# The inputs' first transform as plain-float32 products on two 64-row halves, placed around the response products

## The chip, the cores and the metric

One core of one Trainium2 chip runs the whole kernel. The metric is the device time of one execution in microseconds; lower is better. The kernel before takes 1110.36 us (median of three runs, 1110.23 to 1110.42).

TensorE is called PE below, its weight loads PEld, VectorE DVE, ScalarE ACT, GpSimd POOL and SyncE SP, as in the profile. The queues of these engines run in order.

## The reference

The layer normalizes its input once and adds three things:

```python
x = A_u                                   # 1 x 2048 x 576
xn = _layernorm(x, axis=-1)
return x + _A_ref(xn, ...) + _B_ref(xn, B_w1, B_w2)
# _B_ref: silu(xn @ w1) @ w2,  w1 576 x 4608, w2 4608 x 576
# _A_ref: K[d,l] = Re sum_n C[d,n] exp(dt[d] A[d,n] l) dt[d] B[d,n]
#         y[:,d] = causal convolution of xn[:,d] with K[d,:], plus xn * Dskip
```

So there is a feed-forward branch (two large products with a SiLU between them), and a convolution of 2048 steps per channel, which the reference does with a Fourier transform of length 4096.

## The kernel before, in words

**Feed-forward branch** (`ffn`, lines 257 to 446). The rows are worked in two halves of 1024, each half in two blocks of 512; the 4608 hidden columns in nine chunks of four tiles of 128. `up` (line 321) makes one 128 x 512 tile of the hidden layer from 14 products (lines 331 to 333), then ACT takes the SiLU (line 339) and a rounded copy (line 340), and DVE the remainder (line 342). `down` (line 344) multiplies back in 24 products of 288 columns for each 128 rows (line 357), and DVE adds the result to `acc` (line 361). Every operand is split into a high and a low part of type float32r, and three of the four part products are made.

**Convolution branch** (`side`, line 863, a generator that `weave`, line 33, advances beside the feed-forward steps at fractions of the whole). It goes in stages:

- Layer norm, transposes, preparation of the exponentials (up to about 160 us).
- `kgen` (line 584), 36 chunks of 16 channels: ACT and DVE make tables `S` and `C` of damped sines and cosines (lines 653 to 676). At every second chunk (odd `i`) PE makes the responses from two chunks' tables, 64 plain-float32 products of 64 columns on 128 x 32 column tiles (`kp`, line 696). ACT copies them out (`kt`, line 703). Eight plain-float32 products of 128 columns on 64-row halves then make the first transform of the responses (`z`, line 711, stationary `kt`, moving `f1`), ACT copies the result into `stage` (line 719), and every second time it goes to DRAM.
- `spread` (line 145) makes the first transform of the normalized inputs in the same stretch of time. It is advanced one step by each chunk of `kgen` from the third on (lines 920 to 923). A step takes one of 16 tiles `j` and one half `m` of its rows: ACT rounds 64 rows to float32r into `sp` (line 156), DVE puts the remainder into the other 64 rows (line 157), and for each of two column halves of 288, PE makes two products (lines 161 and 162) with the high and the low part of a doubled matrix `s1`. ACT copies the result to `u1` (line 163), and POOL issues its store to `d1u` (line 164).
- `spectral` (line 730) and `tail` (line 785) do the rest of the convolution (`mm3`, line 821; `add_conv`, line 838, with products `py` of 64-row halves on 64 x 32 tiles, line 847).

**What sets the order.** The tile framework's scheduler orders each engine's queue when the program is built; `high_priority` moves an instruction ahead, and `behind` (line 142, `issue_after`) keeps it behind a named one. What is built is a fixed queue for each engine. The pool `pss` has three PSUM buffers for all small products of the convolution branch; `up` of line 918 has one buffer for `xr`, `u1` and `sp`.

Of the kernel before, what the change touches and what calls it, by code (L numbers as in the profile page):

```python
# [11 lines left out]
F32 = mybir.dt.float32  # L12
F32R = mybir.dt.float32r
# [6 lines left out]
P = 128  # L20
L = 2048
D = 576
NS = 128
FF = 4608
NJ = 16
NKT = 4
HD = D // 2
# [16 lines left out]
def kernel(  # L44
# [11 lines left out]
    w1: bass.AP,  # L56
    w2: bass.AP,
    cident: bass.AP,
    cs1: bass.AP,
    cf1: bass.AP,  # L60
    cm23: bass.AP,
    cs4: bass.AP,
# [3 lines left out]
    nc = tc.nc  # L66
# [73 lines left out]
    pins = {}  # L140

    def behind(ins):
        return tc.issue_after(ins) if ins is not None else nullcontext()

    def spread(up):

        s1 = up.tile([P, 2, P], F32R, name="s1", bufs=1)
        nc.gpsimd.dma_start(s1, cs1)
        for j in range(NJ):
            src = up.tile([P, D], F32, tag="xr", name="xr")  # L150
            nc.sync.dma_start(src, dxn[:, j])
            for m in range(2):
                lo, hi = slice(64 * m, 64 * m + 64), slice(64 - 64 * m, 128 - 64 * m)
                u1 = up.tile([P, D], F32, tag="u1", name="u1")
                sp = up.tile([P, D], F32R, tag="sp", name="sp")
                nc.scalar.copy(sp[lo, :], src[lo, :])
                nc.vector.tensor_sub(sp[hi, :], src[lo, :], sp[lo, :])
                for h in range(2):
                    hs = slice(h * HD, (h + 1) * HD)
                    pu = pss.tile([P, 512], F32, tag="pss", name="pu")  # L160
                    nc.tensor.matmul(pu[:, :HD], s1[:, 0, :], sp[:, hs], start=True, stop=False)  # L161
                    nc.tensor.matmul(pu[:, :HD], s1[:, 1, :], sp[:, hs], start=False, stop=True)  # L162
                    nc.scalar.copy(u1[:, hs], pu[:, :HD])
                nc.gpsimd.dma_start(
                    d1u.rearrange("(p m j) d -> m j p d", m=2, j=NJ)[m, j], u1)
                yield j

    def load_x(j, pool, tag, engines):
# [412 lines left out]
            v.tensor_mul(wt[:, :, k + 1], wt[:, :, k], ex[:, 3 * D:])  # L581
        nc.sync.dma_start(dmag, wt)

    def kgen():
        fT, phiT = kf["f"], kf["phi"]
        with tc.tile_pool(name="kg", bufs=1) as kg:
            CH = 8
# [58 lines left out]
            for i in range(NCK):  # L646
                th = nxt
                pk, ak = pw[:, i % 2], al[:, :, i % 2]
                c65 = kg.tile([P, W, 65], F32, tag="c65", name="c65")
                S = kg.tile([P, W, 96], F32, tag="S", name="S", bufs=2)  # L650
                C = kg.tile([P, W, 96], F32, tag="C", name="C", bufs=2)
                mag = C
                nc.scalar.activation(c65, th, AF.Identity, bias=magic)  # L653
                nc.vector.scalar_tensor_tensor(th, c65, MAGIC, th, op0=ALU.subtract, op1=ALU.subtract)  # L654
                nc.scalar.activation(c65, th, AF.Abs)  # L655
                nc.scalar.activation(th, th, AF.Sin, scale=TWO_PI)
                nc.scalar.activation(c65, c65, AF.Sin, scale=-TWO_PI, bias=halfpi)
                for g in range(2):
                    gs = slice(g * CH, (g + 1) * CH)
                    nc.vector.tensor_mul(  # L660
                        mag[:, gs, 0:32].rearrange("n d (x y) -> n d x y", y=4),
                        pk[:, gs, 0, :].unsqueeze(3).broadcast_to([P, CH, 8, 4]),
                        ak[:, g].unsqueeze(2).broadcast_to([P, CH, 8, 4]))
                nc.vector.tensor_mul(
                    mag[:, :, 32:96].rearrange("n d (x y) -> n d x y", y=8),
                    pk[:, :, 1, :].unsqueeze(3).broadcast_to([P, W, 8, 8]),
                    pk[:, :, 2, :].unsqueeze(2).broadcast_to([P, W, 8, 8]))
                if i + 1 < NCK:
                    nxt = head(i + 1)
                    if i % 2 == 1:  # L670
                        al = powers(i + 1)
                for dst, t, sg in ((S, th, -1.0), (C, c65, 1.0)):
                    ov3 = dst.rearrange("n d (x y) -> n d x y", y=32)[:, :, 0:3:2, :]
                    mv3 = mag.rearrange("n d (x y) -> n d x y", y=32)[:, :, 0:3:2, :]
                    nc.vector.tensor_mul(ov3, t[:, :, 0:64].rearrange("n d (x y) -> n d x y", y=32), mv3)
                    nc.vector.scalar_tensor_tensor(dst[:, :, 32:64], t[:, :, 64:32:-1], sg, mag[:, :, 32:64],  # L676
                                                   op0=ALU.mult, op1=ALU.mult)
                tabs.append((S, C))
                if i % 2 == 0:
                    yield (i + 1) / NCK  # L680
                    continue

                kp = pss.tile([P, 512], F32, tag="pss", name="kp")
                first = None
                for e in (1, 0):
                    S, C = tabs[e]
                    for gl in range(2):
                        for gp_ in range(2):
                            o = e * 256 + (gl * 2 + gp_) * 64
                            for q in range(4):  # L690
                                ch = gp_ * CH + gl * 4 + q
                                dst = kp[32 * q:32 * q + 32, o:o + 64]
                                begins = e == 1 and gl == 0 and gp_ == 0
                                with tc.high_priority(), behind(None if begins else first):
                                    for n, t in enumerate((C, S)):
                                        mm = nc.tensor.matmul(dst, t[:, ch, :32], t[:, ch, 32:],  # L696
                                                              start=begins and n == 0, stop=True,
                                                              tile_position=(0, 32 * q), skip_group_check=True)
                                if begins:
                                    first = mm.ins  # L700
                tabs = []
                kt = kg.tile([P, 512], F32, tag="kt", name="kt")
                nc.scalar.copy(kt, kp)

                z = [pss.tile([P, 512], F32, tag="pss", name="z") for _ in range(2)]
                first = None
                for eg in range(4):
                    for h in (1, 0):
                        rows = slice(64 * h, 64 * h + 64)
                        with tc.high_priority(), behind(first):  # L710
                            mm = nc.tensor.matmul(z[h][:, eg * P:(eg + 1) * P], kt[rows, eg * P:(eg + 1) * P], f1[rows],  # L711
                                                  start=True, stop=True, tile_position=(64 * h, 0))
                        first = first or mm.ins
                r = (i - 1) % NRUN
                if r == 0:
                    stage = kg.tile([P, 64, NRUN * CH], F32, tag="stage", name="stage")
                sv = stage[:, :, r * CH:(r + 2) * CH].rearrange("p k (e h c) -> p h e k c", h=2, c=2)
                for h in range(2):
                    nc.scalar.copy(sv[:, h], z[h].rearrange("p (e k c) -> p e k c", e=4, c=2))
                if r == NRUN - 2:  # L720
                    d0 = (i // NRUN) * NRUN * CH
                    kv = d1k.rearrange("(k n) (g d) -> g n k d", n=64, g=2)
                    for gp_ in range(2):
                        nc.sync.dma_start(kv[gp_, :, :, d0:d0 + NRUN * CH], stage[gp_ * 64:(gp_ + 1) * 64])
                yield (i + 1) / NCK
# [137 lines left out]
    def side():  # L863
# [3 lines left out]
        with tc.tile_pool(name="kf", bufs=1) as kfp:  # L867
# [49 lines left out]
            nc.sync.dma_start(vt, cv)  # L917
            with tc.tile_pool(name="up", bufs=1) as up:
                sp = spread(up)
                for n, at in enumerate(kgen()):  # L920
                    if n > 1:
                        next(sp, None)
                    yield marks[0] + at * (marks[1] - marks[0])
                for _ in sp:
                    pass
# [31 lines left out]
def _constants():  # L957
# [2 lines left out]
    n1 = np.arange(32)  # L960
    th = 2 * np.pi * np.outer(n1, k1 + 0.25) / 32
    cs = np.stack([np.cos(th), np.sin(th)], 2)
    s1 = np.zeros((2, 2, 32, 32, 2, 2), f8)
    f1 = np.zeros((2, 2, 32, 32, 2, 2), f8)
    for q in range(2):
        s1[:, q, :, :, :, q] = cs
        f1[:, q, :, :, :, q] = cs
    s4 = np.broadcast_to(cs.transpose(2, 1, 0) / L, (2, 2, 32, 32)).reshape(P, 32)
    s1 = np.stack(_hi_lo(s1.reshape(P, P)), 1)
    f1 = f1.reshape(P, P)  # L970
    n2 = np.arange(64)
    k2 = np.arange(64)
# [17 lines left out]
    v = np.broadcast_to(v, (P, 69))  # L990
    r = {
        "cident": np.eye(P),
        "cs1": s1,
        "cf1": f1,
        "cm23": m23,
        "cs4": s4,
# [26 lines left out]
```

## Time and profile before

| | |
|---|---|
| time, median of 3 runs | 1110.36 us |
| the profiled execution: span from the first to the last instruction | 1108.2 us |
| PE busy | 1102.2 us, 99% |
| DVE busy | 916.6 us, 83% |
| ACT busy | 706.9 us, 64% |
| POOL busy | 72.1 us, 7% |
| PE products (instructions in the trace) | 9167 |
| granted TensorE clock | full in every slice |

The profile gives the profiled execution no time besides its span; the median of the runs is 2.16 us above that.

A product is recorded from where it starts to where its result is out, so the records of successive products overlap, and the mean duration of one is more than the time that it takes up on PE. That time, called its turn below, is read from the starts of successive products, or from a piece of the chain of waits divided by its count. One plain-float32 product makes two records of weight load and two of product, called its two passes.

### The profile page before, as it was taken

The numbers are of one execution on the slowest core, as the hardware profiler recorded it, in microseconds if no ns is written. First come the engines' busy times: TensorE is split into PE (matmuls) and PEld (weight loads), VectorE is DVE, ScalarE is ACT, GpSimd is POOL, SyncE is SP. The second block draws the span as 40 slices with busy tenths as digits, with TensorE's granted clock in tenths as the row PEclk, the third lists the DMA queues.
The fourth block names the chain that finished last, engine by engine and source line by source line (L and its number), as shares of the span: only waits on it lengthen the run. The fifth ranks groups of instructions, "written<-read, shape, count | busy, mean of one in ns | idle before, by whom it ended". The sixth has DMA issues, their size and how long they took to land.

```text
span 1108.2 us, 22917 instructions
## 1 busy us (share of the span) xinstructions
PE 1102.2 (99%) x9167; PEld 997.5 (90%) x9167; DVE 916.6 (83%) x1543; ACT 706.9 (64%) x1222; POOL 72.1 (7%) x129
## 2 busy tenths in 40 slices
PE   9999999999999999999999999999999999999998
PEld 7989998899998899899999989999999999999887
DVE  7799899999999999999999737787778778784433
ACT  4564466676677676677867536877777878774210
POOL 1100000000000000011000000000000000000111
PEclk9999999999999999999999999999999999999999
DMA  9745512525252525264744173554544455434983
GB/s 270 190 123 160 152 50 61 120 73 131 77 121 83 116 72 118 77 174 154 206 122 103 45 179 109 162 167 123 156 145 152 138 149 170 129 107 127 241 224 87
DMA packets 175755, 148.56 MB, mean 134 GB/s; under 512 B 111088, under 2 KB 142592, under 8 KB 175520
## 3 DMA queue, kind: packets, MB, share of 16 engines
q1 hardware_dynamic: 165328, 112.63, 38.7%
q0 software_dynamic: 9568, 33.62, 9.6%
q8 instruction: 72, 1.18, 0.5%
q10 hardware_dynamic: 752, 0.85, 0.3%
q14 instruction: 35, 0.29, 0.1%
HBM read 102.53 MB, written 44.61 MB: 133 GB/s over the span
## 4 chain that ended last, share of the span: by engine, by line
PE 98%; DMA 1%; DVE 1%; SPq 0%; issue 0%; DVEq 0%
PE po L357 42%; PE ph L331 35%; PE kp L696 3%; PE ph L332 3%; PE ph L333 3%; PE pu L826 2%; PE pb L826 2%; PE pk L826 2%; PE z L711 2%; PE pu L161 1%; PE py L847 1%; DMA acc<-in_A_u_dram 1%; PE pu L162 1%; PE pt L124 0%; DVE w1l L295 0%; PE ptk L490 0%
## 5 line engine op out<-in xcount | busy, mean ns | idle before, releaser
L357 PE MATMUL po<-w2l,gh 128*128 128x288 f32 x1152 | 338.5, 295 | 0.0
L357 PE MATMUL po<-w2h,gl 128*128 128x288 f32 x1152 | 336.4, 295 | 0.0
L357 PE MATMUL po<-w2h,gh 128*128 128x288 f32 x1152 | 336.1, 295 | 0.0
L357 PEld LDWEIGHTS po<-w2h,gh 128*128 128x128 f32 x1152 | 215.2, 188 | 7.7 <-issue 2.8
L357 PEld LDWEIGHTS po<-w2l,gh 128*128 128x128 f32 x1152 | 215.9, 188 | 5.1 <-issue 0.5
L357 PEld LDWEIGHTS po<-w2h,gl 128*128 128x128 f32 x1152 | 215.4, 188 | 0.9
L339 ACT ACTIVATE gf<-ph 128x512 f32<-128x512 f32 (+1 forms) x148 | 86.4, 584 | 143.8 <-PE ph L333 134.8
L331 PE MATMUL ph<-xh,w1l 128*128 128x512 f32 (+1 forms) x592 | 161.3, 385 | 0.0
L331 PE MATMUL ph<-xh,w1h 128*128 128x512 f32 (+1 forms) x592 | 161.3, 387 | 0.0
L331 PE MATMUL ph<-xl,w1h 128*128 128x512 f32 (+1 forms) x592 | 161.1, 385 | 0.0
L361 DVE TENSOR_TENSOR acc<-po,acc 128x288 f32<-128x288 f32 x288 | 126.2, 451 | 37.0 <-PE po L357 35.6
L342 DVE TENSOR_TENSOR gl<-gf,gh 128x512 fp32r<-128x512 f32 (+1 forms) x148 | 99.0, 672 | 64.6 <-ACT gh L340 63.8
L331 PEld LDWEIGHTS ph<-xh,w1l 128*128 128x128 f32 x592 | 108.0, 188 | 20.0
L331 PEld LDWEIGHTS ph<-xl,w1h 128*128 128x128 f32 x592 | 107.9, 188 | 19.8
L331 PEld LDWEIGHTS ph<-xh,w1h 128*128 128x128 f32 x592 | 104.5, 188 | 16.7 <-ACT x L133 0.5
L340 ACT CAST gh<-gf 128x512 fp32r<-128x512 f32 (+1 forms) x148 | 89.5, 608 | 9.5 <-PE po L357 6.6
L653 ACT ACTIVATE c<-th,magic 128x1040 f32<-128x1040 f32 x36 | 42.1, 1168 | 37.9 <-DVE C L676 28.0
L655 ACT ACTIVATE c<-th 128x1040 f32<-128x1040 f32 x36 | 38.7, 1075 | 33.6 <-DVE th L654 33.6
L314 ACT CAST w2h<-w2r 128x576 fp32r<-128x576 f32 x72 | 47.0, 671 | 17.7 <-PE po L357 14.9
L295 DVE TENSOR_TENSOR w1l<-w1r,w1h 128x640 fp32r<-128x640 f32 x72 | 56.9, 817 | 0.2
L332 PE MATMUL ph<-x,w1h 128*128 128x512 f32 (+1 forms) x148 | 57.0, 386 | 0.0
L333 PE MATMUL ph<-x,w1l 128*128 128x512 f32 (+1 forms) x148 | 56.9, 385 | 0.0
(185 smaller groups left out, 1828.8 us busy)
## 6 DMA issues: line engine op xcount, KB each, us to landing
w2r<-in_B_w_dram SPq DMA_DIRECT2D x72, 288.0 KB, 3.8
w1r<-in_B_w_dram SPq DMA_DIRECT2D x35, 512.0 KB, 3.8
d1u<-u POOLq DMA_DIRECT2D x32, 288.0 KB, 2.5
d1k<-stage SPq DMA_DIRECT2D x18, 512.0 KB, 6.8
ur<-d1u SPq DMA_DIRECT2D x32, 288.0 KB, 3.7
kr<-d1k SPq DMA_DIRECT2D x32, 288.0 KB, 2.9
d<-yo POOLq DMA_DIRECT2D x32, 288.0 KB, 4.0
ys<-d SPq DMA_DIRECT2D x32, 288.0 KB, 11.8
```

The lines of the kernel that those rows point to most:

```text
L295: pins["w1l"] = nc.vector.tensor_sub(l1, src, h1).ins
L314: pins["w2h"] = nc.scalar.copy(h2, r2).ins
L331: nc.tensor.matmul(ph, w[:, kt, :], v[:, kt, a:e], start=n + kt == 0, stop=False)
L332: nc.tensor.matmul(ph, h1[:, 4, :], x4[:, a:e], start=False, stop=False)
L333: pins["pe"] = nc.tensor.matmul(ph, l1[:, 4, :], x4[:, a:e], start=False, stop=True).ins
L339: nc.scalar.activation(gf, ph, AF.Silu)
L340: pins["gh"] = nc.scalar.copy(gh, gf).ins
L342: pins["gl"] = nc.vector.tensor_sub(gl, gf, gh).ins
L357: pins["pe"] = nc.tensor.matmul(po[:, :HD], G[blk, t][g][:, js], W2[half, c, t][w][:, hs], start=n == 0, stop=n == 3 * FT - 1).ins
L361: nc.vector.tensor_add(acc[j][:, hs], po[:, :HD], acc[j][:, hs])
L653: nc.scalar.activation(c65, th, AF.Identity, bias=magic)
L826: nc.tensor.matmul(dst, st, mv[:, hs], start=n == 0, stop=n == 3 * len(terms) - 1)
```

## The change

`s1` and its load, the float32r split of the inputs (`sp`) and the paired high and low products go. Each tile `j` is now multiplied as it is, in plain float32, by the matrix `f1` that the response transform uses: rows 0 to 63 (`m` = 0) and rows 64 to 127 (`m` = 1) are two products of 64 rows by 128 columns with 288 moving columns, at tile positions 0 and 64, into two PSUM buffers. A step of `spread` is now one column half `h` of one `j` (32 steps as before), and holds one such pair. `u1` holds both `m` and gets two buffers.

`kgen` now advances `spread` itself: one step ahead of the run of `kp` products and one behind it, at every odd `i` from 3 on. `behind` puts the first pair after the latest feed-forward product, the run after the first pair, and the second pair after the run.

```diff
     def spread(up):
-        s1 = up.tile([P, 2, P], F32R, name="s1", bufs=1)
-        nc.gpsimd.dma_start(s1, cs1)
         for j in range(NJ):
             src = up.tile([P, D], F32, tag="xr", name="xr")
             nc.sync.dma_start(src, dxn[:, j])
-            for m in range(2):
-                lo, hi = slice(64 * m, 64 * m + 64), slice(64 - 64 * m, 128 - 64 * m)
-                u1 = up.tile([P, D], F32, tag="u1", name="u1")
-                sp = up.tile([P, D], F32R, tag="sp", name="sp")
-                nc.scalar.copy(sp[lo, :], src[lo, :])
-                nc.vector.tensor_sub(sp[hi, :], src[lo, :], sp[lo, :])
-                for h in range(2):
-                    hs = slice(h * HD, (h + 1) * HD)
-                    pu = pss.tile([P, 512], F32, tag="pss", name="pu")
-                    nc.tensor.matmul(pu[:, :HD], s1[:, 0, :], sp[:, hs], start=True, stop=False)
-                    nc.tensor.matmul(pu[:, :HD], s1[:, 1, :], sp[:, hs], start=False, stop=True)
-                    nc.scalar.copy(u1[:, hs], pu[:, :HD])
-                nc.gpsimd.dma_start(
-                    d1u.rearrange("(p m j) d -> m j p d", m=2, j=NJ)[m, j], u1)
+            u1 = up.tile([P, 2, D], F32, tag="u1", name="u1", bufs=2)
+            for h in range(2):
+                hs = slice(h * HD, (h + 1) * HD)
+                pu = [pss.tile([P, 512], F32, tag="pss", name="pu") for _ in range(2)]
+                last = pins["small"]
+                for m in (1, 0):
+                    rows = slice(64 * m, 64 * m + 64)
+                    with tc.high_priority(), behind(last):
+                        mm = nc.tensor.matmul(pu[m][:, :HD], f1[rows], src[rows, hs], start=True, stop=True,
+                                              tile_position=(64 * m, 0))
+                    last = pins["small"] = mm.ins
+                for m in range(2):
+                    nc.scalar.copy(u1[:, m, hs], pu[m][:, :HD])
+                if h:
+                    for m in range(2):
+                        nc.gpsimd.dma_start(d1u.rearrange("(p m j) d -> m j p d", m=2, j=NJ)[m, j], u1[:, m])
                 yield j
...
+                pins["small"] = pins["pe"]
+                if i > 1:
+                    next(sp, None)
+                first = pins["small"]
                 kp = pss.tile([P, 512], F32, tag="pss", name="kp")
-                first = None
...
-                                with tc.high_priority(), behind(None if begins else first):
+                                with tc.high_priority(), behind(first):
...
                 nc.scalar.copy(kt, kp)
-
+                pins["small"] = mm.ins
+                if i > 1:
+                    next(sp, None)
                 z = [pss.tile([P, 512], F32, tag="pss", name="z") for _ in range(2)]
...
-                for n, at in enumerate(kgen()):
-                    if n > 1:
-                        next(sp, None)
+                for at in kgen(sp):
                     yield marks[0] + at * (marks[1] - marks[0])
```

More of the change, by code (lines that the diff above doesn't have):

```diff
@@ L58 @@
     cident: bass.AP,
-    cs1: bass.AP,
     cf1: bass.AP,
@@ L582, in natural, with kgen @@
         nc.sync.dma_start(dmag, wt)
-    def kgen():
+    def kgen(sp):
         fT, phiT = kf["f"], kf["phi"]
@@ L962, in _constants @@
     cs = np.stack([np.cos(th), np.sin(th)], 2)
-    s1 = np.zeros((2, 2, 32, 32, 2, 2), f8)
     f1 = np.zeros((2, 2, 32, 32, 2, 2), f8)
     for q in range(2):
-        s1[:, q, :, :, :, q] = cs
         f1[:, q, :, :, :, q] = cs
     s4 = np.broadcast_to(cs.transpose(2, 1, 0) / L, (2, 2, 32, 32)).reshape(P, 32)
-    s1 = np.stack(_hi_lo(s1.reshape(P, P)), 1)
     f1 = f1.reshape(P, P)
@@ L992, in _constants @@
         "cident": np.eye(P),
-        "cs1": s1,
         "cf1": f1,
```

## The prediction

> **What bounds the kernel now.** I read the page first, for the busy shares, and then the chain of waits by line.
>
> ```profile
> span 1108.2 us, 22917 instructions
> PE 1102.2 (99%) x9167; PEld 997.5 (90%) x9167; DVE 916.6 (83%) x1543; ACT 706.9 (64%) x1222; POOL 72.1 (7%) x129
> ...
> by line: PE po L357 41.7%; PE ph L331 35.4%; PE kp L696 3.2%; PE ph L332 3.0%; PE ph L333 2.9%; PE pu L826 2.3%; PE pb L826 2.3%; PE pk L826 2.3%; PE z L711 1.8%; PE pu L161 1.1%; PE py L847 0.9%; DMA acc<-in_A_u_dram 0.8%; PE pu L162 0.8%;
> ```
>
> The chain is nearly all PE. A PE that is 99% busy may still hide short waits, so I asked for the stretch in which the change lies (160 to 645 us: PE, PEld, DVE, ACT and POOL busy, granted clock, DMA) and for the list of waits of PE.
>
> ```profile
> 160.00:645.00 485.00, 485.00 (x5149) 437.53 (x5149) 461.71 (x690) 334.62 (x504) 21.52 (x39) 1.00 0.40 107
> ...
> PE pz L879 <- DVE zero L874: 1.3, 1, 1.3
> PE pt L124 <- DVE xn L202: 0.4, 2, 0.2
> ```
>
> In those 485 us PE has no idle time, at the full clock (1.00); the two waits are of the start. DVE works for 461.7 us of it and ACT for 334.6, but PE waits for neither. So here time is won or lost only in PE's own queue: by the turns of products, by changes of tile mode, and by waits that the change adds.
>
> **Prices.** Two pieces of the chain in order of time, the timeline of PE around one visit to the 64-row mode, the same around one group of `py`, and the durations (min/median/max) of lines 711 and 847.
>
> ```profile
> 365.29 3.18 PE po L357 x24
> 368.70 2.74 PE ph L331 x12
> ...
> 174.23 0.39 PE L331 MATMUL ph<-xh,w1h 128*128 128x512 f32 x1
> 174.55 1.16 PE L711 MATMUL z<-f,kt 64*128 64x128 f32 x16
> 175.64 0.40 PE L161 MATMUL pu<-sp,s 128*128 128x288 f32 x1
> 175.88 0.30 PE L162 MATMUL pu<-sp,s 128*128 128x288 f32 x1
> ...
> 1080.49 0.29 PE L357 MATMUL po<-w2h,gl 128*128 128x288 f32 x1
> 1080.71 1.22 PE L847 MATMUL py<-ys,s 64*32 64x288 f32 x32
> 1081.86 0.73 PE L331 MATMUL ph<-xh,w1h 128*128 128x512 f32 x2
> ...
> L711 PE MATMUL z<-f,kt x288: 272/272/374, 174.5 to 643.0; 64*128 64x128 f32 x144
> ...
> L847 PE MATMUL py<-ys,s x256: 402/403/428, 1032.0 to 1097.0; 64*32 64x288 f32 x128
> ```
>
> - *A float32r product of 288 columns* has a turn of 3.18 / 24 = 0.1325 us, one of 512 columns 2.74 / 12 = 0.228.
> - *A visit to 64-row mode.* The 512-column product of 174.23 has had its turn at 174.46. L162 starts at 175.88; had L161 had one plain turn before it, PE would have been free for L161 at 175.75. So the visit cost 1.29 us.
> - *What of it is streaming.* The 16 records are eight products of two passes. The last record starts at 174.55 + 1.16 - 0.27 = 175.44. The first took 0.374 instead of 0.272, 0.10 of waiting for its weights. If the two halves run side by side there are eight rounds, seven of them between 174.65 and 175.44: 0.113 us each. That is 128 columns in 0.113, about half the rate of float32r (512 columns in 0.228), which fits a plain-float32 pass; one after another each record would have half of that, the full float32r rate. The durations decide: 128 to 288 columns lengthen a record by 403 - 272 = 131 ns, 0.82 ns a column, and float32r takes (0.228 - 0.1325) / 224 = 0.43 ns. So a pass has half the float32r rate, and the halves do run side by side.
> - *A switch.* Eight rounds are 0.90 of the 1.29 us. The other 0.39 is entering and leaving, 0.195 each: PE stands between the last product of one mode and the first of the next, and the first product's weights are not there ahead of it (0.10).
> - *A pass of 288 columns* in 64-row mode: 0.113 + 0.131 = 0.244 us. The `py` group checks it. It has 16 products on eight tiles, so four rounds. From 1080.49 + 0.1325 = 1080.62 to the second `ph` product (1081.86 + 0.73 - 0.39 = 1082.20) less a turn of 0.228, it cost 1.35; four rounds are 0.98, and 0.37 is left for two switches.
>
> **The change, part by part.**
>
> *Removed from PE:* 64 L161 and 64 L162, 128 x 0.1325 = 17.0 us. That their chain share (1.1% + 0.8% of 1108.2, 21.1 us) is more comes from L161 standing behind `z` in 17 rounds and taking over the leaving of it; the next product will take that over.
>
> *Added to PE, streaming:* 64 plain-float32 products of 64 rows. In the built order of the changed kernel 31 of the 32 pairs stand together and one is parted by eight feed-forward products, so there are 33 stretches of two passes: 33 x 2 x 0.244 = 16.1 us. At this point the change is about even: two passes at half the rate, two products at a time, against two products at full rate.
>
> *Added to PE, switches:* this decides. Counted in the built orders, the tile mode of PE's queue changes 96 times before and 145 times after. `kp` needs 128 x 32, the pairs 64 x 128, the feed-forward 128 x 128. Only 8 of the 16 first pairs lie directly against the run (14 to 77 feed-forward products stand between in the others), 15 second pairs begin directly behind it, and three `z` groups are now parted in two. A first pair that stands free costs two switches; a pair against the run costs one more than the run alone. 49 x 0.195 = 9.6 us.
>
> The trace has no border between the 64-row mode and `kp`'s. Below, such a border could cost nothing (the float32 work runs on); above, as much as a whole visit's overhead, 0.39. There are 23 of them (8 + 15). I take 0.195, as `z` shows for a change of rows, for both its directions; the ends are -4.5 and +4.5 us. The Trainium skill (TensorEngine Tiling (Array Packing), Key Properties) says that changing the tiling mode, not just the tile, drains TensorE. By that rule all 23 borders pay and the sum stays as it is; the trace agrees where it can be seen, with 0.39 us for a visit, and no run here yet shows that border.
>
> Another rule bears on the removal. The skill's page TensorE: Matmul & The Clock Gate (Back-to-back issue gap) gives N / 2.4 + 2.5 ns, an estimate of 122.5 ns for 288 columns, by which 15.7 us would go and the sum would be 1.3 us higher; the chain shows 132.5 ns, and that decides.
>
> *Removed elsewhere:* 32 roundings on ACT, 32 subtractions on DVE, one load on POOL.
>
> ```profile
> L156 ACT CAST sp<-xr 64x576 fp32r<-64x576 f32 x32 | 21.5, 673 | 6.0 <-DMA xr<-dxn 2.9 <-PE pu L162 2.7
> L157 DVE TENSOR_TENSOR sp<-xr,sp 64x576 fp32r<-64x576 f32 x32 | 24.1, 753 | 1.0
> L163 ACT COPY u<-pu 128x288 f32<-128x288 f32 x64 | 24.2, 400 | 10.5 <-PE pu L162 10.4
> ```
>
> That is 21.5 us of ACT and 24.1 us of DVE, worth nothing while PE has no idle time to give back. The 64 copies to `u1` (0.40 each), the 16 loads of `xr` on SP and 32 stores on POOL stay.
>
> *Added waits.* The second pair stands behind the run in PE's queue and needs the buffers of the first pair, so ACT's two copies of that pair. Behind it on PE are some 17 feed-forward products and `z`; all of them would stand too. I looked at how far ahead ACT and DVE are there, around the run at 222 us (timelines of DVE, ACT, PE; then the chain).
>
> ```profile
> 217.67 0.69 DVE L676 SCALAR_TENSOR_TENSOR C<-c,C 128x512 f32<-128x512 f32 x1
> ...
> 218.45 1.17 ACT L653 ACTIVATE c<-th,magic 128x1040 f32<-128x1040 f32 x1 [0.85 <-DVE C L676]
> 223.79 1.06 ACT L656 ACTIVATE th<-th 128x1040 f32<-128x1040 f32 x1
> 228.14 0.58 ACT L703 COPY kt<-kp 128x512 f32<-128x512 f32 x1
> ...
> 222.03 0.34 PE L696 MATMUL kp<-C 128*32 128x64 f32 x8
> ...
> 224.09 4.97 PE po L357 x36
> ```
>
> The run lasts from 222.03 to 224.09, 2.06 us. The built order of ACT mostly has the L653 operation (1.17) and the two copies (0.80) between: 1.97 us, covered even if L653 begins only when the first pair is done; in the trace it began 3.6 us ahead of the run. I cost this wait at nothing; without the cover it is the first rival. The tables were done at 218.36, 3.7 us ahead, so `kp`'s own wait has slack. On SP the load of the next `xr` now waits for PE's second pair instead of DVE; the table bases and weight loads queue behind it, but the tile is wanted only a round later (18 rounds in the stretch of 485 us, 27 us each), so nothing.
>
> **Sum:** 16.1 + 9.6 - 17.0 = +8.7 us. The profiled span of 1108.2 becomes 1116.9; with the 2.16 us by which the median of 1110.36 lies above that span, **1119.1 us**.
>
> **Rivals.**
>
> 1. *PE waits for ACT at the second pairs.* For it: the `kt` copy began 4.05 us after its run had ended, at 228.14, since ACT was working off its queue. Against: the copies stand ahead of the long sines. If ACT comes to the copies one such operation (1.06) late, 1.97 + 1.06 - 2.06 = 0.97 us are lost; at five to fifteen pairs that is 4.9 to 14.6 us: 1124.0 to 1133.7.
> 2. *Borders with `kp` are free:* 23 x 0.195 = 4.5 us less, 1114.6. For it: no row shows such a border. Against: both modes differ in rows and columns.
> 3. *The pairs don't run side by side,* so the change doesn't do what it says: 31 x 0.488 = 15.1 us more, 1134.2. Against: the eight rounds of `z`.
> 4. *Not slower: PE goes into and out of the 64-row mode for nothing,* weights loaded ahead. With all 49 switches at 0 the sum is 16.1 - 17.0 = -0.9, 1109.5 us. It decides at (2.2 + 0.9) / 49 = 0.06 us a switch. Against: 0.195 in `z`, which also goes from and to float32r products.
>
> **How the numbers follow.** The forecast, 1116.5 to 1122 with small waits, has 0.70; rival 1 0.13; rival 2 0.08; rival 3 0.03; rival 4 0.04, and 0.02 is for a gain that no row shows. 0.2%, about 2.2 us, is what a measurement here can tell from no change. Only rival 4 lies within it: faster 0.02, same 0.04, slower 0.94. The range takes in the forecast, rival 2 and the low end of rival 1: 1114.5 to 1124.0 leaves out just under 2 in 10.
>
> **What would show it.** Right: PE still without idle time between 160 and 645 us; the pair's two starts within some 10 ns and its first record about 0.10 us longer than its second pass's 0.40; a free pair's visit of 0.88 us (0.488 + 0.39), a pair against the run adding 0.68. Wrong: starts half a microsecond apart (rival 3); PE idle ahead of the second pair with ACT as releaser (rival 1); a `kp` border well under 0.2 us (rival 2); the feed-forward products slower or faster than 0.1325 and 0.228 us, which I take as unchanged.

## The result, and the profile after

The changed kernel takes **1123.26 us** (median of four runs, 1122.72 to 1123.62); the kernel before took 1110.31 us beside it (four runs, 1110.23 to 1110.42). The ratio is 1.0115, with a 95% interval of 1.0103 to 1.0127: 12.95 us slower, inside the forecast's range, 4.2 us above its value and above the narrower 1116.5 to 1122 that had most of the chance. The profiled execution took 1123.62 us, its span 1121.8.

First the page of the kernel after: the span, the busy shares, the chain by line.

```profile
span 1121.8 us, 22820 instructions
...
PE 1114.9 (99%) x9167; PEld 994.4 (89%) x9167; DVE 892.1 (80%) x1511; ACT 688.2 (61%) x1190; POOL 71.4 (6%) x128
...
PE po L356 37%; PE ph L330 31%; PE ph L332 3%; PE ph L331 3%; PE kp L698 2%; PE pu L830 2%; PE pb L830 2%; PE pk L830 2%; PE z L715 2%; PE pu L157 1%; PE py L851 1%; DMA acc<-in_A_u_dram 1%; DVE acc L360 1%; DMA xl<-dxt 1%; DVE th L653 1%
```

PE is 99% busy as before. Lines of the code have moved: the pair is L157 now, `z` L715, `kp` L698, the feed-forward products L330 to L332 and L356. The same stretch by time (PE, PEld, DVE, ACT, POOL busy, clock, DMA):

```profile
160.00:645.00 485.00, 484.93 (x4950) 422.80 (x4949) 432.45 (x650) 310.35 (x463) 21.41 (x39) 1.00 0.41 106
```

And all waits of PE that the trace lists in the kernel after:

```profile
PE pt L123 <- DVE xn L201: 1.3, 2, 1.1
PE pz L883 <- DVE zero L878: 1.3, 1, 1.3
```

PE still has no idle time in the stretch and the clock is full; DVE is busy for 29 us less there and ACT for 24, and PE gains nothing by it. (The operations taken out were 24.1 and 21.5 us; the rest is work that now lies later.) The stretch now holds 4950 product records where it held 5149, out of 9167 in both kernels: the same count takes longer in PE's own queue. Where, the timeline of PE shows; each row is a run of equal records with its start, its length and its count.

```profile
188.36 0.29 PE L356 MATMUL po<-w2h,gl 128*128 128x288 f32 x1
188.58 0.76 PE L157 MATMUL pu<-xr,f 64*128 64x288 f32 x4
189.27 0.50 PE L330 MATMUL ph<-xl,w1h 128*128 128x512 f32 x1
189.60 0.62 PE L330 MATMUL ph<-xh,w1l 128*128 128x512 f32 x2
...
201.25 0.29 PE L356 MATMUL po<-w2l,gh 128*128 128x288 f32 x1
201.47 1.49 PE L715 MATMUL z<-f,kt 64*128 64x128 f32 x16
202.89 0.40 PE L356 MATMUL po<-w2h,gl 128*128 128x288 f32 x1
203.13 0.29 PE L356 MATMUL po<-w2l,gh 128*128 128x288 f32 x1
...
220.59 0.29 PE L356 MATMUL po<-w2h,gl 128*128 128x288 f32 x1
220.81 0.76 PE L157 MATMUL pu<-xr,f 64*128 64x288 f32 x4
221.50 0.34 PE L698 MATMUL kp<-C 128*32 128x64 f32 x8
...
223.49 0.76 PE L157 MATMUL pu<-xr,f 64*128 64x288 f32 x4
224.18 0.50 PE L332 MATMUL ph<-x,w1l 128*128 128x512 f32 x1
224.51 0.29 PE L356 MATMUL po<-w2h,gh 128*128 128x288 f32 x1
...
359.49 0.29 PE L356 MATMUL po<-w2l,gh 128*128 128x288 f32 x1
359.72 1.16 PE L715 MATMUL z<-f,kt 64*128 64x128 f32 x8
360.80 0.40 PE L356 MATMUL po<-w2h,gl 128*128 128x288 f32 x1
361.04 0.30 PE L356 MATMUL po<-w2h,gh 128*128 128x288 f32 x1
```

A visit is read as in the prediction: from the end of the last full product's turn to the second full product, less a turn.

- *A free pair* (188.58): from 188.36 + 0.1325 = 188.49 to 189.60 - 0.228 = 189.37, so 0.88 us.
- *A pair, the run, a pair* (220.81): from 220.72 to 224.51 - 0.228 = 224.28, so 3.56 us. A run alone took 39.53 us in 18 visits before, 2.20 each. Each pair against the run adds 0.68.
- *A `z` group* (201.47): from 201.38 to 203.13 - 0.1325 = 203.00, so 1.61 us. Before it was 1.29 for the same 16 records.
- *Half a `z` group* (359.72, eight records): from 359.62 to 360.91, 1.29 us. Half the products cost as much as the whole group did, and the other half comes later, at 362.63, for as much again.

All visits between 160 and 700 us, summed the same way, are 62.72 us before (`kp` 39.53, `z` 23.19) and 92.81 after (`kp` and the pairs 64.09, `z` 28.72). With the 17.0 us that went, that is 92.81 - 62.72 - 17.0 = **+13.1 us**, against 12.95 measured. The spans differ by 13.6; 0.9 of that is the wait of `pt` in the first 20 us (1.3 us, 0.4 before), long before the first pair.

So `z`, which the change does not touch, costs 5.5 us more. In the queue as built, 10 of its 18 groups go on alternating between rows 64 to 127 (H) and rows 0 to 63 (l). Five run H H H l H l l l, at 1.61 us (in the trace the second half starts 0.33 us behind the first, against 0.007 where they alternate, and that late start is the whole 0.32); three are parted into H H H H and, later, l l l l, at twice 1.29. 5 x 0.32 + 3 x 1.29 = 5.5.

### The profile page after: what moved, and what is told of

It is laid out like the page before. It is cut to its first block, busy times and chain, and to the rows that moved or that the text cites. A ratio compares the mean times of both kernels' runs of the same rounds, so it can differ in the third digit from the quotient of the medians.

```text
span 1121.8 us, 22820 instructions
## 1 busy us (share of the span) xinstructions
PE 1114.9 (99%) x9167; PEld 994.4 (89%) x9167; DVE 892.1 (80%) x1511; ACT 688.2 (61%) x1190; POOL 71.4 (6%) x128
## 4 chain that ended last, share of the span: by engine, by line
PE 86%; DVE 6%; issue 4%; DMA 2%; ACT 1%; POOL 0%; SPq 0%; DVEq 0%; POOLq 0%
PE po L356 37%; PE ph L330 31%; PE ph L332 3%; PE ph L331 3%; PE kp L698 2%; PE pu L830 2%; PE pb L830 2%; PE pk L830 2%; PE z L715 2%; PE pu L157 1%; PE py L851 1%; DMA acc<-in_A_u_dram 1%; DVE acc L360 1%; DMA xl<-dxt 1%; DVE th L653 1%
## 5 line engine op out<-in xcount | busy, mean ns | idle before, releaser
L356 PE MATMUL po<-w2h,gh 128*128 128x288 f32 x1152 | 337.6, 296 | 0.0
L356 PE MATMUL po<-w2l,gh 128*128 128x288 f32 x1152 | 337.6, 295 | 0.0
L356 PE MATMUL po<-w2h,gl 128*128 128x288 f32 x1152 | 335.5, 296 | 0.1
L356 PEld LDWEIGHTS po<-w2h,gh 128*128 128x128 f32 x1152 | 215.4, 188 | 10.3 <-issue 5.5
L356 PEld LDWEIGHTS po<-w2l,gh 128*128 128x128 f32 x1152 | 215.7, 188 | 5.3 <-issue 0.8
L356 PEld LDWEIGHTS po<-w2h,gl 128*128 128x128 f32 x1152 | 214.6, 188 | 3.8 <-issue 1.5
L330 PE MATMUL ph<-xl,w1h 128*128 128x512 f32 (+1 forms) x592 | 161.6, 386 | 0.0
L330 PE MATMUL ph<-xh,w1l 128*128 128x512 f32 (+1 forms) x592 | 161.4, 386 | 0.0
L330 PE MATMUL ph<-xh,w1h 128*128 128x512 f32 (+1 forms) x592 | 160.9, 388 | 0.0
L330 PEld LDWEIGHTS ph<-xh,w1l 128*128 128x128 f32 x592 | 107.9, 188 | 21.1 <-issue 0.8
L330 PEld LDWEIGHTS ph<-xl,w1h 128*128 128x128 f32 x592 | 107.9, 188 | 20.7 <-issue 0.4
L330 PEld LDWEIGHTS ph<-xh,w1h 128*128 128x128 f32 x592 | 104.3, 188 | 19.3 <-issue 3.2
L674 DVE TENSOR_TENSOR S<-th,C 128x1024 f32<-128x1024 f32 x36 | 44.0, 1222 | 25.0 <-ACT th L655 24.8
L315 DVE TENSOR_TENSOR w2l<-w2r,w2h 128x576 fp32r<-128x576 f32 x72 | 53.5, 752 | 4.7 <-ACT w2h L313 4.6
```

The costliest lines, as they stand in the source:

```text
L315: pins["w2l"] = nc.vector.tensor_sub(l2, r2, h2).ins
L330: nc.tensor.matmul(ph, w[:, kt, :], v[:, kt, a:e], start=n + kt == 0, stop=False)
L356: pins["pe"] = nc.tensor.matmul(po[:, :HD], G[blk, t][g][:, js], W2[half, c, t][w][:, hs], start=n == 0, stop=n == 3 * FT - 1).ins
```

## The experiments

Theory A, under every expectation: PE's queue alone sets the time, and its price is made of turns, of switches at 0.195 us, and of the order of the halves in `z`. The rivals stand in each expectation. "Before" is always the kernel before on the same chip in the same batch, 1110.1 to 1110.5 us.

### The order of the halves alone

```diff
 # in the kernel before, nothing else changed
-                first = None
-                for eg in range(4):
-                    for h in (1, 0):
+                last = None
+                for h in (1, 0):
+                    for eg in range(4):
                         rows = slice(64 * h, 64 * h + 64)
-                        with tc.high_priority(), behind(first):
+                        with tc.high_priority(), behind(last):
...
-                        first = first or mm.ins
+                        last = mm.ins
```

> The kernel before with one edit: the eight z products in the order of their halves, four of rows 64 to 127, then four of rows 0 to 63, each tied behind the one before it, in all 18 groups. Same products, same switches. Theory A (the order of the halves has a price of its own, the products of one half running one after another): a group ordered so took 0.55 us more than an alternating one in the run with float32r products at the new places, so 18 x 0.55 = 9.9 us: 1120.3 us. Theory B (the z part of the difference is waits for ScalarE's copies, not order): within 1 us of before, 1110 to 1111.5 us.

Measured: 1122.29 us (1120.02 to 1125.51), ratio 1.0102 (1.0077 to 1.0127). The timeline of PE around the first group of this kernel:

```profile
174.63 0.39 PE L331 MATMUL ph<-xh,w1h 128*128 128x512 f32 x1
174.94 1.71 PE L711 MATMUL z<-f,kt 64*128 64x128 f32 x16
176.58 0.40 PE L161 MATMUL pu<-sp,s 128*128 128x288 f32 x1
176.82 0.29 PE L162 MATMUL pu<-sp,s 128*128 128x288 f32 x1
```

From 174.86 to 176.69, 1.83 us, where the alternating group took 1.29. The 18 groups together take 33.03 us instead of 23.19, +9.84, as A has it, and PE has no listed wait between 160 and 700 us. The runs at 1120.0 and 1120.5, whose mean granted clock is 1.000, are that price alone. The profiled execution (1124.06) also has a wait of 2.8 us of `py` for its load `ys` near 1041 us, and behind it, from 1045.4 to 1048.8 us, half the granted clock, which costs another 1.7; its mean clock is 0.998, and so is that of the run at 1125.5. Same products, same data, same number of switches: the order alone costs 10 us. So the order of the halves has a price of its own.

### A buffer of its own for the second half of z

```diff
-                z = [pss.tile([P, 512], F32, tag="pss", name="z") for _ in range(2)]
+                z = [pool.tile([P, 512], F32, tag=t, name="z") for pool, t in ((pss, "pss"), (ps2, "ps2"))]
```

> The changed kernel with one edit: the second half of z takes its PSUM buffer from the pool of the feed-forward sums (ps2), so that it waits for no copy of a pair. In the built queue all 18 z groups then alternate their two halves again (the changed kernel has 9 that don't), and two second pairs and two z groups come to lie against each other. Theory A (switches and the order of the halves make the whole difference): priced from the rows of the two traces, PE's visits cost 24.0 us more than before instead of 30.0, so 1110.3 + 7.0 = 1117.3 us. Theory B (the 4 us over the forecast are waits of PE for ScalarE's copies or VectorE's tables): a z buffer of its own changes little, 1121 to 1123 us.

Measured: 1129.61 us (1128.2 to 1130.16), ratio 1.0170 (1.0156 to 1.0184). All 18 groups alternate again, and the 15 that stand by themselves take 1.29 us each (the other three share a visit with pairs). So the buffer was what parted the halves: `pss` has three, and in the built order the second half stood behind ACT's copies of the second pair. (The expectation counts nine groups that don't alternate in the kernel after; its trace has eight that take longer.) But the kernel got slower. The list of waits of PE in this kernel:

```profile
PE po L356 <- DVE acc L360: 3.9, 2, 2.2
PE pu L157 <- DMA xr<-dxn: 2.4, 1, 2.4
PE ph L330 <- ACT w1h L292: 1.6, 1, 1.6
```

`ps2` holds the feed-forward sums `po`. The timeline of DVE shows why PE waits for one there (its product starts at 293.98, 2.2 us late):

```profile
291.39 0.68 DVE L675 SCALAR_TENSOR_TENSOR C<-c,C 128x512 f32<-128x512 f32 x1
292.00 1.23 DVE L636 TENSOR_TENSOR th<-vt,fT 128x1040 f32<-128x1040 f32 x1
293.15 0.49 DVE L630 TENSOR_TENSOR pw<-pw 128x192 f32<-128x192 f32 x1
293.48 0.44 DVE L360 TENSOR_TENSOR acc<-po,acc 128x288 f32<-128x288 f32 x1
```

The sum stands behind a row of table operations. And after the wait comes a second loss, seen in the windows (the clock is the third number from the end):

```profile
288.00:295.00 7.00, 4.80 (x36) 4.57 (x35) 7.00 (x11) 2.87 (x6) 0.00 (x0) 1.00 0.34 120
295.00:298.40 3.40, 3.40 (x17) 3.40 (x16) 2.67 (x7) 3.39 (x6) 0.00 (x0) 0.50 0.02 5
```

For 3.4 us the granted clock is half, which costs 1.7 us; it happens again at 581.7 us. 1117.3 by A, 7.9 us of listed waits and 3.4 of half clock make 1128.6, against 1129.61. A's price for `z` holds; the cure is not free.

### Every z product behind the one before it

```diff
-                first = None
+                last = None
                 for eg in range(4):
                     for h in (1, 0):
...
-                        with tc.high_priority(), behind(first):
+                        with tc.high_priority(), behind(last):
...
-                        first = first or mm.ins
+                        last = mm.ins
```

> The changed kernel with each z product tied behind the one before it, so that the two halves must alternate; all buffers stay as in the changed kernel. In the built queue 10 of the 18 z groups stand whole and alternate; in the other 8 the first product stands alone, feed-forward products follow, and the other seven come later. Theory A: such a parted group costs a switch pair and two passes more, 0.61 us, against 0.32 or 1.29 for the orders that it replaces: 12.0 us over before, 1122.5 us. Theory E (the waits of PE for VectorE's sums in the two runs with borrowed ps2 buffers come from the borrowing): no such wait here, so 1122 to 1123.5. Theory F (they come with any new order of the queues): waits of some us here too, 1125 us or more.

Measured: 1124.06 us (1123.52 to 1127.23), ratio 1.0124 (1.0106 to 1.0142). The order is forced but the buffer is as scarce as before, so now in seven groups (the expectation counts eight) the first H product runs alone, feed-forward products follow, and the rest comes in a second visit: at 201.4 us the two visits take 1.88 us where the kernel after took 1.61. PE has no wait for DVE's sums here; the only one behind the early stages is `py`'s for `ys`, 3.3 us in the profiled execution (1127.23), with half clock for 3.4 us behind it. With A's 1122.5 that makes 1127.5. The other three runs, 1123.5 to 1124.4, lie 1 to 2 us above A's price, between theories E and F, and what they lose is not shown. That no sum is waited for speaks for E: those waits come with borrowing `ps2`.

### The pairs inside the visits of z

```diff
-                pu = [pss.tile([P, 512], F32, tag="pss", name="pu") for _ in range(2)]
+                pu = [pool.tile([P, 512], F32, tag=t, name="pu")
+                      for pool, t in (((ps2, "ps2") if h else (pss, "pss")), (ps2, "ps2"))]
...
-                pins["small"] = pins["pe"]
-                if i > 1:
-                    next(sp, None)
-                first = pins["small"]
+                first = pins["pe"]
...
-                        with tc.high_priority(), behind(first):
+                        with tc.high_priority(), behind(last):
...
-                        first = first or mm.ins
+                        last = pins["small"] = mm.ins
+                    if eg in (0, 3) and i > 1:
+                        next(sp, None)
+                        last = pins["small"]
```

> The changed kernel with the same 64 plain-float32 products, but moved to the response transform, which uses the same 64-row mode: the first pair stands between the first two z products and the other six, the second pair behind the last; the second pair and one product of the first take their buffers from ps2. In the built queue 29 of the 32 pairs lie whole inside a visit, three are parted. Theory A: a pair inside a visit costs its two passes alone, 0.49 us; priced so, 18.3 us are added and 17.0 removed: 1111.6 us. Theory C (plain float32 is what is dear, wherever it stands): as the changed kernel less its z part, 1117 us or more. If the borrowed buffers make the feed-forward sums wait, PE shows idle time and the time lies above 1111.6.

Measured: 1127.29 us (1125.95 to 1129.1), ratio 1.0154 (1.0140 to 1.0168). A visit of this kernel in the timeline of PE:

```profile
201.39 0.39 PE L332 MATMUL ph<-x,w1h 128*128 128x512 f32 x1
201.71 0.49 PE L710 MATMUL z<-f,kt 64*128 64x128 f32 x4
202.03 0.65 PE L158 MATMUL pu<-xr,f 64*128 64x288 f32 x4
202.52 0.83 PE L710 MATMUL z<-f,kt 64*128 64x128 f32 x12
203.19 0.66 PE L158 MATMUL pu<-xr,f 64*128 64x288 f32 x4
203.77 0.50 PE L333 MATMUL ph<-x,w1l 128*128 128x512 f32 x1
204.11 0.86 PE L331 MATMUL ph<-xh,w1h 128*128 128x512 f32 x3
```

From 201.39 + 0.228 = 201.62 to 204.11 - 0.228 = 203.88: 2.26 us for `z` and two pairs, and 1.29 + 2 x 0.488 = 2.27. Between the products of one mode no switch is paid here, and a pair costs its streaming price. The price of 1111.6 is not reached all the same; the list of waits of PE has the reason:

```profile
PE po L357 <- DVE acc L361: 3.5, 5, 1.8
PE py L849 <- DMA ys<-d: 2.3, 1, 2.3
PE z L710 <- ACT kt L703: 2.0, 3, 0.7
PE po L357 <- ACT u L162: 1.9, 3, 1.4
```

These are 9.7 us of the 17.5 by which the profiled execution (1129.1) is above A; with the smaller waits, read from the starts of the products on both sides of each gap, it is about 16, and one stretch of half clock costs 1.7. The expectation's last sentence, waits by the borrowed buffers, is what came; theory C has such a time too, but its reason, a high price of plain float32 wherever it stands, does not fit the 2.26 us.

### The old products at the new places

```diff
 # in the kernel before; kgen also advances spread ahead of and behind the run of kp, as in the change (left out here)
-                    nc.tensor.matmul(pu[:, :HD], s1[:, 0, :], sp[:, hs], start=True, stop=False)
-                    nc.tensor.matmul(pu[:, :HD], s1[:, 1, :], sp[:, hs], start=False, stop=True)
+                    for n in range(2):
+                        with tc.high_priority(), behind(pins["small"]):
+                            mm = nc.tensor.matmul(pu[:, :HD], s1[:, n, :], sp[:, hs], start=n == 0, stop=n == 1)
+                        pins["small"] = mm.ins
```

> The kernel before with its float32r products, two steps around each run of kp as in the change (one step ahead, one behind, each with the same ties and priority). No switch is added, since float32r products run in the mode of the feed-forward products. Theory A: only the 6 z groups that lose their alternation in the built queue cost, 5 x 0.32 + 0.89 = 2.5 us: 1112.8 us. Theory B (the new places make PE wait): 1116 us or more, with idle time of PE around kp.

Measured: 1114.14 us (1113.9 to 1114.53), ratio 1.0035 (1.0022 to 1.0047). Six `z` groups have lost their alternation here too (five at 1.61 us, one at 1.84), together 2.2 us, and PE waits 0.6 us for the table `C` at `kp` and 0.4 for `w2h`. With small gaps beside these that is the measured +3.7. So the places alone, with no new mode and no new product, cost 3.7 us through the order of `z` and some waits. The other 9.3 us of the change come with the plain-float32 pairs: 7.6 for the pairs themselves (24.6 less 17.0), the rest by what they do to the order of `z`.

### The new products at the old places

```diff
 # the kernel after, spread advanced one step per chunk as before, its pairs tied to nothing but each other
-                last = pins["small"]
+                last = None
...
-                    with tc.high_priority(), behind(last):
+                    with tc.high_priority() if last else nullcontext(), behind(last):
...
+                for n, at in enumerate(kgen()):
+                    if n > 1:
+                        next(sp, None)
```

> The changed kernel with its pairs advanced by every chunk as before the change, not tied to kp. In the built queue every tile j has one pair parted, its first product directly behind z and its second alone, and the other pair alone, whole. Theory A: per tile 0.49 + 0.88 + 0.88 = 2.25 us, 36.0 us in all less 17.0 removed, and z alternates: about 19.5 us over before, 1129.9 us, with any waits of PE and half-clock stretches on top. Theory C (only the plain-float32 products count, not where they stand): as the changed kernel, 1123 us.

Measured: 1132.04 us (1131.51 to 1133.94), ratio 1.0195 (1.0180 to 1.0210). The scheduler parts 17 of the pairs: one product hangs on a `z` visit (1.78 us instead of 1.29, so a lone product costs as much as a pair), the other makes a visit of its own. The visits sum to 100.17 us, 20.5 more than before net of the 17.0 removed, near A's 19.5; 1110.5 + 20.5 leaves 1.1 us of the median open. The run agrees with the price, not with theory C, and the placement in the change is better than this one.

### The second pair behind z

```diff
-                pins["small"] = mm.ins
-                if i > 1:
-                    next(sp, None)
-                z = [pss.tile([P, 512], F32, tag="pss", name="z") for _ in range(2)]
+                z = [pool.tile([P, 512], F32, tag=t, name="z") for pool, t in ((pss, "pss"), (ps2, "ps2"))]
-                first = None
+                last = None
...
-                        with tc.high_priority(), behind(first):
+                        with tc.high_priority(), behind(last):
...
-                        first = first or mm.ins
+                        last = mm.ins
+                pins["small"] = last
+                if i > 1:
+                    next(sp, None)
```

> The changed kernel with the second pair tied behind the last z product instead of behind the run of kp, and the second half of z in a ps2 buffer. In the built queue all second pairs lie against z, z alternates, and two z groups lie directly behind kp. Theory A: the second pairs cost 0.49 us each, 4.6 us over before, 1115.0 us; the two z groups behind kp have to wait for the copy kt, 0.93 us each as such groups did in the run with both pairs at z, so 1116.9, and any further wait shows as idle time of PE on top. Theory C: 1121 us or more without such waits.

Measured: 1126.11 us (1124.7 to 1127.07), ratio 1.0137 (1.0122 to 1.0152). A `z` with a pair behind it takes 1.775 us (14 visits), as priced; the first wait in the list of PE's waits is again that for DVE's sums:

```profile
PE po L356 <- DVE acc L360: 4.3, 4, 2.5
```

The profiled execution (1126.82) lies 9.9 us above A's 1116.9; the waits for these sums, for `ys` (1.7) and for `w1h` (1.3), and a stretch of half clock at 295.5 us (1.7), are 9.0 of it.

All three kernels that take buffers from `ps2` wait for DVE's sums (3.5 to 4.3 us); the kernel after and the four variants above that leave `ps2` alone (halves apart, pinned, old products, old places) have no such wait.

### What PE's 17 us are worth at all

```diff
 # the kernel after without the pair's products
-                for m in (1, 0):
...
-                        mm = nc.tensor.matmul(pu[m][:, :HD], f1[rows], src[rows, hs], start=True, stop=True,
...
-                    nc.scalar.copy(u1[:, m, hs], pu[m][:, :HD])
+                    nc.scalar.copy(u1[:, m, hs], src[:, hs])
```

> The changed kernel without the 64 plain-float32 products: ScalarE copies the inputs themselves to u1, so the first transform of the inputs is left out and the output is not the layer's. Theory A: PE loses the 30.0 us of visits that the change added, and the 17.0 us of float32r products are gone as well: 1110.3 - 17.0 = 1093.3 us, all z groups alternating. Theory B: PE's queue is not all that counts; the tables or copies would hold it at 1096 us or more, and PE would show idle time.

Measured: 1107.14 us (1104.15 to 1109.16), ratio 0.997 (0.996 to 0.998): a gain of 3.3 us, not 17. But the edit moved more than it took out. Nothing ties the copies to a place any more, and all 64 of them start between 137 and 224 us, where the kernel after has them from 190 to 630. The longest wait of PE, ACT's queue ahead of it, and two windows:

```profile
PE po L348 <- ACT gh L331: 2.8, 1, 2.8
```

```profile
166.27 1.43 ACT L153 COPY u<-xr 128x288 f32<-128x288 f32 x4 [1.65 <-DMA xr<-dxn]
167.61 1.14 ACT L331 CAST gh<-gf 128x512 fp32r<-128x512 f32 x2
```

```profile
130.00:225.00 95.00, 87.85 (x753) 76.36 (x752) 76.64 (x119) 70.28 (x135) 17.13 (x32) 1.00 0.67 199
225.00:700.00 475.00, 473.29 (x4806) 425.57 (x4805) 422.71 (x649) 296.19 (x430) 7.86 (x13) 1.00 0.36 93
```

The `gh` that PE waits for stands behind four copies that had themselves waited for their load. PE is idle for 7.15 us in the 95 us that hold the copies and for 1.7 us in the 475 us after them. Behind the stretch, the profiled execution (1109.02) has 2.3 us of `py`'s wait and 3.4 us of half clock. So theory B's idle time is there, but most of it lies among the bunched copies and loads, which are an effect of the experiment. Waits for DVE's sums (2.5 us) arise here without any borrowing, so borrowing is not the only way to them.

### No first transform at all

```diff
 # the kernel after without the pairs and the copies; the inputs go to d1u
-                for m in range(2):
-                    nc.scalar.copy(u1[:, m, hs], pu[m][:, :HD])
...
-                        nc.gpsimd.dma_start(d1u.rearrange("(p m j) d -> m j p d", m=2, j=NJ)[m, j], u1[:, m])
+                        nc.gpsimd.dma_start(d1u.rearrange("(p m j) d -> m j p d", m=2, j=NJ)[m, j], src)
```

> The changed kernel without the inputs' first transform: no products and no copies, the loaded tiles themselves are stored to d1u, so the output is not the layer's. PE loses 17.0 us against before and z alternates. Theory A in its plain form (only PE's queue counts in both directions): 1093.4 us. Theory D (PE's lead over VectorE and ScalarE is small: VectorE is busy for 462 of 485 us there, so a shorter queue of PE turns into waits): 1100 to 1108 us with waits of PE for VectorE and ScalarE of 7 us or more in the stretch from 140 to 660 us. The earlier run without products still had 64 copies that waited for loads; here ScalarE has none.

Measured: 1106.8 us (1104.96 to 1110.24), ratio 0.997 (0.996 to 0.998). The time is the rival's, the mechanism is not. The longest wait of PE, then what SP's queue did:

```profile
PE po L344 <- ACT w2h L301: 8.5, 1, 8.5
```

```profile
187.09 13.77 SPq L148 DMA_DIRECT2D xr<-dxn  x3
200.96 0.85 SPq L292 DMA_DIRECT2D w2r<-in_B_w_dram  x2
```

SP issues the load of the weights `w2r` at 200.96, after the queue has stood 13.77 us on three loads of `xr`, whose tile was not free; PE waits 8.5 us and then has half clock for 6.8 us (200.9 to 207.7). This is an effect of the experiment, since the tile is held by its store there. It alone, 8.5 us and 3.4 for the half clock, is 11.9 of the 12.4 us by which the profiled execution (1105.78) lies above A. So neither run shows that DVE and ACT would hold up a shorter queue of PE: they gained 3.3 and 3.7 us of 17, and much of what they lost lies where the experiment had bunched copies and loads. What 17 us of PE are worth with everything else in its place stays open.

## Why the prediction was right or wrong, point by point

- *PE bounds the stretch, and time freed on DVE and ACT is worth nothing:* right. No wait is listed for the kernel after between 160 and 645 us.
- *Removed, 17.0 us; the feed-forward products unchanged:* right. The chain of the kernel after has 24 products of `po` in 3.18 us, as before, and 13.1 us by this sum against 12.95 measured leaves no room for another effect of size.
- *A pair streams for 0.488 us, side by side:* right. The first record of a pair is 0.507 us long and the two starts lie 7 ns apart; the free visit takes 0.88. The visit of `z` and two pairs gives 0.488 once more. Rival 3 falls.
- *A border between the pairs and `kp` costs one switch:* right, 0.68 us for each pair against the run. 23 free borders would have left 0.49. Rival 2 falls. The trace now agrees, at this border too, with the rule of the Trainium skill (TensorEngine Tiling (Array Packing), Key Properties) that a change of tiling mode drains TensorE.
- *Pairs and their switches together, 16.1 + 9.6 - 1.2 = 24.5 us:* measured 24.6.
- *The second pairs wait for nothing:* right in this build; rival 1 falls. It does not carry over to other builds: in the three variants that borrow a buffer, PE waits for some 8 to 16 us in all, for DVE's sums first, which the prediction did not consider.
- *Rival 4, switches for nothing:* falls; a free pair takes 0.88 us where 0.488 is streaming.
- *"three `z` groups are now parted in two", 1.2 us:* **this is the step that failed.** It priced the parting as six switches. Measured, `z` costs 5.5 us more. A parted half saves no streaming, since four products of one half take as long as eight in alternation: 1.29 us more for each of the three, not 0.39. And five further groups were not parted but reordered, 0.32 us each. Both stood in the built order that the prediction read; it counted changes of mode there, and not which half each product belongs to. With 5.5 in place of 1.2 the sum is +13.0, and 1110.36 + 13.0 = 1123.4.
- *The range:* in part luck. The measured 1123.26 lies above the forecast's 1116.5 to 1122. It is inside 1114.5 to 1124.0 only because the top was stretched for the low end of rival 1, waits for ACT, which did not come.

Shown by experiment: the price of the order (halves apart, +9.84 us in the visits, nothing else changed) and that the scarce buffer breaks the alternation (with a buffer from elsewhere all 18 groups alternate). Not shown: a build of the change in which `z` alternates and no new wait arises. By its price it would take 1117.3 us, still 7 us above the kernel before. By price alone only pairs inside the visits of `z` come near it (1111.6), and that build waits. No version that was run beats the kernel before with the whole computation in it.

## What to carry to other kernels

Where PE is the bound, read its built queue twice: once for changes of tile mode, and once for the row half of each product, since here four products of one half took as long as eight of two halves in turn. A placement that holds a scarce PSUM buffer longer changes the order of the products that come next, and that must be priced too. And an experiment that takes work out must leave the rest where it was: here 17 us less on PE gained 3 to 4, but copies and loads had moved as well, so the runs don't tell how close DVE and ACT stand behind PE.

## What the runs showed of the hardware

- Eight plain-float32 products of 128 columns on two 64-row halves take 1.29 us with their two switches when the halves alternate, 1.61 in the order H H H l H l l l, 1.83 as H H H H l l l l, and 2.58 in two visits. In a reordered group the second half starts before the first is through, 0.33 us behind it.
- The half clock came in stretches of 3.4 us or twice that, after short idle times. After 2.2 us of idle time at 291.6 us it came (the windows of the kernel with the borrowed buffer above); after 2.8 us at 165.5 us, in the kernel without the pairs, it did not, and the clock in its window above is 1.00. The Trainium skill (TensorE: Matmul & The Clock Gate, What's actually happening) has free-running windows of about 3.4 us and half clock after at least one idle window; the length of the stretches agrees, but here 2.2 us without a product was enough at one place.
- `py`'s wait for its load `ys`, 1.4 to 3.3 us near 1030 to 1050 us, shows in the profiled execution of seven variants and not in those of before and after. In five of the seven a stretch of half clock follows it. With the halves apart, two of the four runs have a mean clock of 1.000 and are 3.5 to 5.5 us shorter than the two with 0.998, so it seems to come and go between the executions of one kernel; what decides it was not tried.
